# Local attention and a squared-ReLU layer on one core: another order of the opening and of block 0's first layer, with the 256-token products split by x's words

## The chip, the cores and the metric

The kernel runs on one core of one Trainium2 chip. A core has five engines that run their own instruction lists in order and wait for one another by semaphores: TensorE (PE, matrix products; its loads of weights are shown as PEld), VectorE (DVE), ScalarE (ACT), GpSimd (POOL) and SyncE (SP, which here issues nearly all DMA transfers). The metric is the device time of one execution in microseconds (us), as the median of several runs. One further execution was recorded by the profiler, and its records are the trace that the rows below come from.

## The reference, cut to what matters

```python
q, k, v: (8, 8, 576, 64) float32      # batch, heads, sequence, head size
# attention inside chunks of 64 positions
scores = (1 / sqrt(64)) * q_c @ k_c^T          # 64 x 64 in each chunk
attn = exp(scores - max); attn = attn / (attn.sum(-1) + 1e-9)
x = (attn @ v_c), laid out as (4608 tokens, 512)
# the layer
h = x @ w_in            # 512 x 2048
g = s * relu(h) ** 2 + b
out = g @ w_out         # 2048 x 512, float32
```

The weights arrive as 64-bit floats and are turned into 32-bit floats on the chip.

## The kernel before, in words

The first 512 tokens are worked by themselves (class `Layer`), the other 4096 in four blocks of 1024 (class `Block`). To keep float32 accuracy on PE, a matrix product is made of three: each operand is split into a high word and a low word (`hi` and `lo`), and high x high, high x low and low x high are summed. A product of 128 x 128 weights with 512 tokens is one PE instruction of about 0.227 us, one with 256 tokens takes about half. In the blocks of 1024 the first layer is computed with 7 products in place of 8 of half-size operands (steps p1 to p7, copies u, joins c11 to c22, relux and reluy, sqx and sqy). The first 512 tokens use plain products, and the weights come in while these run.

What stands first in time is a hand-written list of step names, `ORDER`. It is executed once from front to end, and each step appends its instructions to the lists of its engines. So the list fixes the order on every engine, and on SP the order in which transfers are issued. The steps that matter here:

- `one` and `two` are the attention groups of the first 256 + 256 tokens, each in halves 0 and 1: load_qk, load_v (512 KB transfers), scores (PE L498), peak, sub, exp, sum, normz, norm (DVE, exp on ACT), transposes (PE L559), copies (ACT L564), values (PE L571), x_hi (ACT L579) and x_lo (DVE L583). `three` to `ten` are later groups of 256 tokens in one piece (scores L395, norm L421, transposes L431, values L456). Groups three to six make the tokens of the first block of 1024: their x words are x11.hi, x21.hi, x21.lo (DVE L625) and so on.
- Weight tiles come in as `load0` to `load15`, each 1 MB (load0 in halves a and b), and each goes through ACT `scale` (L179) and `tail` (L183), DVE `shift` (L189) and `sign` (L191), POOL `add` (L197), ACT `hi` (L201) and DVE `lo` (L205). There are three buffers for them.
- `up<j>` is the first layer's product j of 16 for 512 tokens (L689, 12 products of 512 columns). `up0a` and `up1a` are its first 256 columns (the tokens of group one), `up0b` and `up1b` the second 256 (group two), 12 products of 256 columns each. Then come `relu` (ACT L694), `square` (ACT L701), `g_hi` (ACT L706) and `g_lo` (DVE L710). `down<j>` is the second layer's product j (PE L664, 12 products: 6 into `ps_x`, 6 into `ps_o`). There are two `ps_h` tiles. From j = 2 on, `g_lo` is the last reader of the one that `up` filled, so the `up` after the next waits for it.
- `s_add`, `s_hi` (ACT L245), `s_lo` (DVE L248) make the sums of weights for the 7 products; `in` and `out` store weights; `ring` loads them back.
- `keep_busy<n>` issues n products of a tile of ones with itself, 128 columns each (L131). Their result is read by nobody. The trace shows each as two passes.

In the list before, `keep_busy` stands at six places (7, 3, 8, 7, 4 and 2 products). The first layer starts with up1a, up0a, then `three.scores`, up1b, up0b, up3 and up2, and down0. After the step `nine.scores` in the middle of the list, the lists before and after the change are alike but for the order of a few neighbours up to `p3.4`.

Of the kernel before, what the change touches and what calls it, by code (L numbers as in the profile page):

```python
# [20 lines left out]
one.scores0 one.peak0 s_and_b sb one.sub0 one.exp0 one.scores1 keep_busy7 one.peak1 one.sum0 three.load_v one.sub1
one.normz0 one.norm0 one.exp1 four.load_v tail0b one.transposes0 keep_busy3 one.sum1 one.normz1 one.copies0 one.norm1
tail0a scale0a load2 one.transposes1 four.load_qk shift0a scale0b two.scores0 keep_busy8 one.copies1 sign0a shift0b
add0a two.peak0 two.sub0 hi0a sign0b two.scores1 two.exp0 lo0a add0b two.peak1 one.values0 keep_busy7 two.sum0
# [5 lines left out]
g_lo0 g_hi3 three.norm down0 scale4 g_lo1 hi3 shift4 relu2 g_lo3 three.transposes sign4 square2 g_hi2 down1 load6 lo3  # L30
tail5 scale5 add4 g_lo2 in2 three.copies up4 shift5 hi4 sign5 tail6 load7 four.scores lo4 relu4 scale6 add5 up5 out1
four.peak square4 five.load_qk g_hi4 four.sub hi5 shift6 down2 load8 g_lo4 relu5 sign6 tail7 scale7 lo5 three.values
four.exp add6 in3 square5 up6 four.sum three.x_out g_hi5 shift7 hi6 g_lo5 down3 sign7 relu6 square6 four.normz g_hi6
# [1276 lines left out]
```

## Time and profile before

| what | value |
|---|---|
| time, median of 3 runs | 781.4 us (780.26 to 781.6) |
| profiled execution, its own time | 779.79 us |
| span of that execution in the trace | 777.8 us |
| PE busy | 765.3 us, 98% of the span |
| DVE / ACT / POOL busy | 600.8 / 475.1 / 48.7 us |
| chain that ended last, by engine | PE 83%, DMA 8%, DVE 4%, ACT 3% |

The profiled execution's own time is 2.0 us above its span: the span runs from the first to the last recorded instruction. Its time lies 1.6 us under the median of the three runs. An engine counts as busy while an instruction of it runs; a row of the timeline gives the start of an instruction or of a run of like ones, its duration, the engine, the line of the kernel, the operation, what it writes and reads with the shape, the count, and in brackets the idle time just before it with what ended that idle time.

### The profile page before, as it was taken

Reading aid. Unit: us, or ns where it says so; the run is one execution under the profiler, and the core shown is the slowest. Engines: PE = TensorE matmul, PEld = TensorE weight load, DVE = VectorE, ACT = ScalarE, POOL = GpSimd, SP = SyncE. Lnnn points to the kernel's source line nnn. Section 1 sums busy time; section 2 is a strip of 40 time slices with the busy share of each in tenths; the row PEclk is TensorE's granted clock in tenths of the full one; section 3 lists DMA queues with packets and bytes.
Section 4 is the critical chain, followed back from the end, with each engine's and each line's share of the span. In section 5 each row is a group of like instructions: output and inputs, shape, how many; then the busy total and the mean of one; then the engine's idle time right before and its main releaser. Section 6 shows DMA issues by size and latency. Waiting matters only on the chain.

```text
span 777.8 us, 13753 instructions
## 1 busy us (share of the span) xinstructions
PE 765.3 (98%) x5560; PEld 632.6 (81%) x5560; DVE 600.8 (77%) x799; ACT 475.1 (61%) x657; POOL 48.7 (6%) x23
## 2 busy tenths in 40 slices
PE   6899999999999999999999999999999999999998
PEld 5788887888888888888888888888888888888886
DVE  6988899986479999889888956677998623348773
ACT  4899877867664552776764535667755345575442
POOL 1453440000000000000000000000000000000000
PEclk9999999999999999999999999999999999999999
DMA  9999999677898889999756687765575778876653
GB/s 357 352 357 344 373 302 321 231 248 222 282 386 306 305 287 367 356 321 334 232 184 223 204 319 261 268 248 190 170 236 194 236 265 284 307 256 217 212 193 136
DMA packets 86227, 211.66 MB, mean 272 GB/s; under 512 B 6036, under 2 KB 42388, under 8 KB 75924
## 3 DMA queue, kind: packets, MB, share of 16 engines
q1 hardware_dynamic: 85872, 210.53, 77.8%
q8 instruction: 44, 0.72, 0.4%
q10 hardware_dynamic: 292, 0.26, 0.1%
q14 instruction: 19, 0.16, 0.1%
HBM read 166.72 MB, written 44.04 MB: 271 GB/s over the span
## 4 chain that ended last, share of the span: by engine, by line
PE 83%; DMA 8%; DVE 4%; ACT 3%; issue 1%; SPq 1%; POOL 0%; POOLq 0%; DVEq 0%
PE ps_h L745 22%; PE ps_h L994 17%; PE ps_o L745 17%; PE ps_x L994 8%; PE ps_o L994 4%; PE ps_o L896 3%; PE ps_o L923 3%; DMA raw<-in_w_dram 3%; DMA w_in<-t 3%; PE ps_h L896 1%; PE ps_x L923 1%; PE ps_x L896 1%; PE ps_a L395 1%; DMA w_out<-t 1%; PE ps_x L456 1%; DMA t<-in_qkv_dram 1%
## 5 line engine op out<-in xcount | busy, mean ns | idle before, releaser
L745 PE MATMUL ps_h<-t,raw 128*128 128x512 f32 x672 | 167.2, 391 | 0.0
L964 DVE TENSOR_TENSOR t<-t 128x512 fp32r<-128x512 f32 (+1 forms) x140 | 123.0, 900 | 36.1 <-ACT t L959 36.1
L745 PEld LDWEIGHTS ps_h<-t,raw 128*128 128x128 f32 x672 | 125.5, 188 | 26.3
L994 PE MATMUL ps_h<-t,raw 128*128 128x512 f32 (+1 forms) x588 | 142.4, 385 | 0.0
L764 DVE TENSOR_TENSOR t<-ps_o,u 128x512 f32<-128x512 f32 x96 | 65.5, 687 | 82.2 <-PE ps_o L745 64.9
L994 PEld LDWEIGHTS ps_h<-t,raw 128*128 128x128 f32 x588 | 108.8, 188 | 22.2
L745 PE MATMUL ps_o<-t,raw 128*128 128x512 f32 x480 | 122.0, 390 | 0.0
L959 ACT CAST t<-t 128x512 fp32r<-128x512 f32 (+1 forms) x140 | 102.3, 789 | 16.0 <-DVE t L943 5.8
L745 PEld LDWEIGHTS ps_o<-t,raw 128*128 128x128 f32 x480 | 89.9, 188 | 19.0 <-DVE t L764 0.3
L755 ACT COPY u<-ps_h 128x512 f32<-128x512 f32 x96 | 55.9, 584 | 72.4 <-PE ps_h L745 72.0
L994 PE MATMUL ps_x<-t,raw 128*128 128x512 f32 x288 | 73.2, 390 | 0.0
L808 ACT ACTIVATE t<-t 128x1024 f32<-128x1024 f32 x64 | 67.1, 1052 | 0.2
L994 PEld LDWEIGHTS ps_x<-t,raw 128*128 128x128 f32 x288 | 53.9, 188 | 11.6 <-DVE shift L1166 0.3
L804 ACT ACTIVATE t<-t 128x512 f32<-128x512 f32 (+1 forms) x64 | 54.1, 847 | 12.9 <-DVE t L764 12.8
L197 POOL TENSOR_TENSOR t<-t,raw 128x1024 int32<-128x1024 int32 (+1 forms) x17 | 48.0, 2822 | 66.9 <-DVE t L191 40.7
L998 ACT ACTIVATE u<-ps_h,shift,sb 128x512 f32<-128x512 f32 x18 | 13.1, 781 | 58.2 <-PE ps_h L994 58.2
L689 PE MATMUL ps_h<-x,t 128*128 128x512 f32 (+1 forms) x216 | 47.1, 371 | 1.6 <-DVE x L583 1.6
L689 PEld LDWEIGHTS ps_h<-x,t 128*128 128x128 f32 x216 | 36.8, 188 | 8.8 <-DVE x L583 1.8
L994 PE MATMUL ps_o<-t,raw 128*128 128x512 f32 x144 | 36.5, 389 | 0.0
L443 DVE STREAM_TRANSPOSE pT<-p 32x512 f32<-32x512 f32 x48 | 33.7, 703 | 0.9
L800 ACT ACTIVATE t<-ps_h 128x512 f32<-128x512 f32 x32 | 19.1, 597 | 23.4 <-PE ps_h L745 23.4
L994 PEld LDWEIGHTS ps_o<-t,raw 128*128 128x128 f32 x144 | 27.0, 188 | 5.6
(145 smaller groups left out, 1052.2 us busy)
## 6 DMA issues: line engine op xcount, KB each, us to landing
raw<-w_in SPq DMA_DIRECT2D x42, 1024.0 KB, 6.0
raw<-w_out SPq DMA_DIRECT2D x29, 1024.0 KB, 5.1
raw<-w_sum SPq DMA_DIRECT2D x28, 1024.0 KB, 5.2
raw<-in_w_dram SPq DMA_DIRECT2D x15, 1024.0 KB, 7.7
qk<-in_qkv_dram SPq DMA_DIRECT2D x15, 1024.0 KB, 9.1
w_out<-t SPq DMA_DIRECT2D x16, 512.0 KB, 6.9
t<-w_out SPq DMA_DIRECT2D x16, 512.0 KB, 7.9
w_sum<-t SPq DMA_DIRECT2D x16, 512.0 KB, 7.6
```

The lines of the kernel that those rows point to most:

```text
L197: nc.gpsimd.tensor_tensor(out=i, in0=i, in1=low.bitcast(I32), op=ALU.add)
L443: nc.vector.transpose(out=self.pT[cols, 1 - k], in_=p[rows, k])
L689: nc.tensor.matmul(out=self.ps[j][:, cols], lhsT=w[:, c, :], rhs=x[:, c, :], start=(c == 0 and i == 0), stop=(c == NHP - 1 and i == 2))
L745: nc.tensor.matmul(out=ps, lhsT=w[:, e, :], rhs=y[:, e, :], start=start and e + i == 0, stop=e + i == 3, skip_group_check=not start)
L755: nc.scalar.copy(out=u, in_=self.a[p])
L764: nc.vector.tensor_tensor(out=self.tile(p, h)[:, e, :], in0=ps, in1=u, op=ALU.add)
L804: nc.scalar.activation(out=t, in_=t, func=AF.Relu)
L808: nc.scalar.activation(out=t, in_=t, func=AF.Square)
L896: nc.tensor.matmul(out=self.acc[names[m // 2]][m % 2], lhsT=x, rhs=y, start=j == 0 and q == 0, stop=q == 2, skip_group_check=j > 0)
L959: nc.scalar.copy(out=hi, in_=f)
L964: nc.vector.tensor_tensor(out=lo, in0=f, in1=hi.bitcast(F32), op=ALU.subtract)
L994: nc.tensor.matmul(out=self.acc[name][m][:, cols], lhsT=x, rhs=y[:, cols], start=new and q == 0, stop=q == 2, skip_group_check=not new)
```

## The change

Three things change. The list `ORDER` is rewritten from its start up to the step `nine.scores`. `Layer.up` takes the three products in the order high x high, low weight x high x, high weight x low x (before: the low word of x second, the low word of the weights third), and can issue a part of them. And the four 256-column steps are split: `up<j>a.x` and `up<j>b.x` issue the first two products of each of the four chunks (8 instructions, which read no low word of x), `.y` the third (4 instructions). `keep_busy` stands at four places: 8 products ahead of everything, then 13, 10 and 11. The count of real products is the same.

```diff
 ORDER = """
-one.load_qk0 one.load_qk1 load0b one.load_v load0a two.load_qk0 two.load_qk1 load1 two.load_v three.load_qk
...
-one.x_hi0 two.sub1 load3 hi0b one.x_lo0 two.exp1 lo0b one.values1 keep_busy4 tail1 two.normz0 in0 two.sum1 one.x_hi1
-scale1 two.norm0 two.normz1 two.transposes0 keep_busy2 two.norm1 one.x_lo1 shift1 two.copies0 two.values0 sign1
-two.transposes1 two.x_hi0 two.copies1 add1 two.x_lo0 up1a scale2 tail2 two.values1 shift2 up0a hi1 sign2 two.x_hi1
-three.scores lo1 add2 two.x_lo1 in1 three.peak scale3 up1b tail3 three.sub up0b open_o load4 relu1 shift3 hi2 up3
...
+keep_busy8 one.load_qk0 one.scores0 one.peak0 s_and_b sb one.sub0 one.exp0 one.load_qk1 load0b two.load_qk0 load0a two.load_qk1
+two.load_v one.load_v load1 three.load_v load2 one.scores1 keep_busy8 keep_busy5 one.peak1 one.sub1 one.sum0 scale0b
...
+two.sub1 one.x_hi0 load3 tail1 two.exp1 hi0b two.normz0 two.norm0 two.sum1 lo0b one.values1 two.transposes0 keep_busy9
+two.normz1 scale1 keep_busy2 two.copies0 tail2 one.x_hi1 shift1 two.norm1 two.values0 sign1 one.x_lo0 one.x_lo1
+two.transposes1 add1 up1a.x up1a.y two.x_hi0 scale2 two.copies1 two.x_lo0 up0a.x two.values1 three.scores up0a.y
+two.x_hi1 hi1 shift2 sign2 add2 two.x_lo1 three.peak three.sub up1b.x up1b.y relu1 scale3 up0b.x up0b.y open_o load5
...
-eight.normz u2.3 s_keep4 eight.norm p2.4 u1.4 eight.turn p6.4 p7.3 c11.4 u2.4 eight.swap0 relux.4 p7.4 u3.3 c22.3 p4.3
-u3.4 eight.swap1 p3.3 ring9 c21.3 sqx.3 p1.5 s_hi5 c12.3 p4.4 ring10 s_lo5 u1.5 reluy.3 p5.4 s_keep5 c21.4 sqy.3
-eight.values nine.scores c22.4 sqx.4 p3.4 eight.x_out nine.load_v nine.peak p6.5 nine.sub s_hi6 ring11 c12.4 p2.5
...
+eight.swap0 relux.4 p7.4 u3.3 c22.3 p4.3 u3.4 ring8 p4.4 p3.3 ring9 c21.3 sqx.3 c12.3 p5.4 eight.values ring10 c21.4
+reluy.3 sqy.3 s_hi5 s_lo5 s_keep5 p1.5 u1.5 nine.scores c22.4 sqx.4 p3.4 eight.x_out nine.load_v nine.peak p6.5
...
-        def up(self, j, cols=slice(0, HALF)):
+        def up(self, j, cols=slice(0, HALF), part=(0, 1, 2)):
...
-                for i, (w, x) in enumerate(((h, xh), (h, xl), (l, xh))):
-                    nc.tensor.matmul(out=self.ps[j][:, cols], lhsT=w[:, c, :], rhs=x[:, c, :],
-                                     start=(c == 0 and i == 0), stop=(c == NHP - 1 and i == 2))
+                for i, (w, x) in enumerate(((h, xh), (l, xh), (h, xl))):
+                    if i in part:
+                        nc.tensor.matmul(out=self.ps[j][:, cols], lhsT=w[:, c, :], rhs=x[:, c, :],
+                                         start=(c == 0 and i == 0), stop=(c == NHP - 1 and i == 2))
...
-        named["up%da" % j], named["up%db" % j] = partial(layer.up, j, first), partial(layer.up, j, second)
+        for h, cols in (("a", first), ("b", second)):
+            named["up%d%s" % (j, h)] = partial(layer.up, j, cols)
+            named["up%d%s.x" % (j, h)], named["up%d%s.y" % (j, h)] = partial(layer.up, j, cols, (0, 1)), partial(layer.up, j, cols, (2,))
```

In the changed file the lines of `Layer` stand one lower: L690 is `up`, L711 is `g_lo`.

First place: PE from the last scores of group two to the first `down`. L498 are scores of one and two, L559 transposes, L571 values, L131 the products of keep_busy (a count of products, not passes), L395 `three.scores`. Before:

```order
L498 MATMUL ps_p<-t 64x64 x16
L571 MATMUL ps_p<-pT,t 64x64 x16
L131 MATMUL ps_h<-t 128x128 x7
L571 MATMUL ps_p<-pT,t 64x64 x16
L131 MATMUL ps_h<-t 128x128 x4
L559 MATMUL ps_a<-ident,t 128x128 x4
L131 MATMUL ps_h<-t 128x128 x2
L571 MATMUL ps_p<-pT,t 64x64 x16
L559 MATMUL ps_a<-ident,t 128x128 x4
L689 MATMUL ps_h<-x,t 128x256 x12
L571 MATMUL ps_p<-pT,t 64x64 x16
L689 MATMUL ps_h<-x,t 128x256 x12
```

In the changed kernel:

```order
L571 MATMUL ps_p<-pT,t 64x64 x16
L559 MATMUL ps_a<-ident,t 128x128 x4
L131 MATMUL ps_h<-t 128x128 x11
L571 MATMUL ps_p<-pT,t 64x64 x16
L559 MATMUL ps_a<-ident,t 128x128 x4
L690 MATMUL ps_h<-x,t 128x256 x20
L571 MATMUL ps_p<-pT,t 64x64 x16
L395 MATMUL ps_a<-t 64x64 x32
L690 MATMUL ps_h<-x,t 128x256 x28
L690 MATMUL ps_h<-x,t 128x512 x24
```

The 11 warming products now stand between group two's two sets of transposes; 20 products of 256 columns (up1a.x, up1a.y, up0a.x) run ahead of the last values and of `three.scores`, and 28 behind.

Second place: DVE around `shift8`, `sign8`, `lo6`, `shift9` and `g_lo7`. L205 is `lo`, L189 `shift`, L191 `sign`, L710 `g_lo`. Before:

```order
L421 TENSOR_TENSOR t<-t,z 128x1024
L205 TENSOR_TENSOR t<-t 128x1024
L189 TENSOR_SCALAR t<-t 128x1024
L205 TENSOR_TENSOR t<-t 128x1024
L191 SCALAR_TENSOR_TENSOR t<-raw,t 128x1024
L189 TENSOR_SCALAR t<-t 128x1024
L710 TENSOR_TENSOR t<-ps_h,t 128x512
```

In the changed kernel:

```order
L421 TENSOR_TENSOR t<-t,z 128x1024
L205 TENSOR_TENSOR t<-t 128x1024
L189 TENSOR_SCALAR t<-t 128x1024
L191 SCALAR_TENSOR_TENSOR t<-raw,t 128x1024
L205 TENSOR_TENSOR t<-t 128x1024
L189 TENSOR_SCALAR t<-t 128x1024
L711 TENSOR_TENSOR t<-ps_h,t 128x512
```

`sign8`, after which POOL may start `add8`, and `lo6` have changed places; `shift9` and `g_lo7` follow as before.

Third place: DVE around `sign12`, `five.norm` (L421) and `x21.lo` (L625), up to the step `lo11` (the last L205 here). Before:

```order
L189 TENSOR_SCALAR t<-t 128x1024
L421 TENSOR_TENSOR t<-t,z 128x1024
L191 SCALAR_TENSOR_TENSOR t<-raw,t 128x1024
L625 TENSOR_TENSOR t<-half,t 128x1024
L710 TENSOR_TENSOR t<-ps_h,t 128x512 x2
L625 TENSOR_TENSOR t<-half,t 128x1024
L189 TENSOR_SCALAR t<-t 128x1024
L205 TENSOR_TENSOR t<-t 128x1024
```

In the changed kernel:

```order
L189 TENSOR_SCALAR t<-t 128x1024
L191 SCALAR_TENSOR_TENSOR t<-raw,t 128x1024
L421 TENSOR_TENSOR t<-t,z 128x1024
L625 TENSOR_TENSOR t<-half,t 128x1024
L711 TENSOR_TENSOR t<-ps_h,t 128x512 x2
L625 TENSOR_TENSOR t<-half,t 128x1024
L189 TENSOR_SCALAR t<-t 128x1024
L205 TENSOR_TENSOR t<-t 128x1024
```

`sign12` now stands ahead of `five.norm`, so two more operations with two operands in the core's memory (the norm and `x21.lo`) follow it. In the same way `sign15` and `lo14` now stand ahead of `six.norm`, and PE's `six.transposes` ahead of `down12`.

## Rows read from the trace of the kernel before

**Rows 1.** Windows: busy us (x instructions) of each engine, granted clock, DMA share, GB/s.
```profile
0.00:36.00 36.00, 27.07 (x459) 24.21 (x460) 28.37 (x46) 22.62 (x32) 10.30 (x11) 1.00 0.94 354
36.00:774.40 738.40, 738.27 (x5103) 608.42 (x5101) 571.90 (x753) 452.47 (x626) 38.37 (x13) 1.00 0.78 269
```

**Rows 2.** Timeline of PE in the opening: start, duration, instruction, idle before.
```profile
6.91 2.65 PE L131 MATMUL ps_h<-t 128*128 128x128 f32 x14
...
22.64 0.69 PE L571 MATMUL ps_p<-pT,t 64*64 64x64 f32 x32 [0.28 <-ACT pT L564]
...
23.68 1.68 PE L689 MATMUL ps_h<-x,t 128*128 128x256 f32 x12
...
30.82 8.47 PE L689 MATMUL ps_h<-x,t 128*128 128x256 f32 x47 [1.60 <-DVE x L583]
39.13 1.67 PE L664 MATMUL ps_x<-t 128*128 128x512 f32 x6
```

**Rows 3.** Timeline of DVE in the opening.
```profile
12.66 0.43 DVE L189 TENSOR_SCALAR t<-t 128x512 uint32<-128x512 uint32 x1 [0.78 <-ACT t L179]
...
20.46 0.68 DVE L529 TENSOR_TENSOR t<-t,z 128x512 f32<-128x512 f32 x1
...
26.05 1.72 DVE L189 TENSOR_SCALAR t<-t 128x1024 uint32<-128x1024 uint32 x1 [0.80 <-ACT t L179]
...
30.08 0.69 DVE L583 TENSOR_TENSOR x<-ps_p,x 128x512 fp32r<-128x512 f32 x1
...
33.08 0.68 DVE L189 TENSOR_SCALAR t<-t 128x1024 uint32<-128x1024 uint32 x1
...
36.07 1.21 DVE L414 TENSOR_REDUCE z<-t 128x16 f32<-128x1024 f32 x1
...
38.69 0.63 DVE L710 TENSOR_TENSOR t<-u,t 128x512 fp32r<-128x512 f32 x1
```

**Rows 4.** The chain that ended last, the transfer of load2.
```profile
11.19 13.63 DMA raw<-in_w_dram
```

**Rows 5.** Timeline of POOL: `add1`, `add8`.
```profile
24.78 2.44 POOL L197 TENSOR_TENSOR t<-t,raw 128x1024 int32<-128x1024 int32 x1 [6.95 <-ACT pT L564]
...
69.15 2.69 POOL L197 TENSOR_TENSOR t<-t,raw 128x1024 int32<-128x1024 int32 x1 [5.59 <-DMA raw<-in_w_dram]
```

**Rows 6.** Timeline of DVE at the second place, `g_lo7` and `sign9`.
```profile
69.45 0.68 DVE L710 TENSOR_TENSOR t<-ps_h,t 128x512 fp32r<-128x512 f32 x1
70.06 2.88 DVE L191 SCALAR_TENSOR_TENSOR t<-raw,t 128x1024 uint32<-128x1024 uint32 x1
```

**Rows 7.** Timeline of PE: `up9`; `up13`; `down12`.
```profile
71.25 2.88 PE L689 MATMUL ps_h<-x,t 128*128 128x512 f32 x12
...
97.73 1.66 PE L689 MATMUL ps_h<-x,t 128*128 128x512 f32 x6
...
115.50 1.52 PE L664 MATMUL ps_x<-t 128*128 128x512 f32 x6
```

**Rows 8.** Timeline of DVE at the third place.
```profile
90.66 1.22 DVE L625 TENSOR_TENSOR t<-half,t 128x1024 fp32r<-128x1024 f32 x1
93.97 1.29 DVE L710 TENSOR_TENSOR t<-ps_h,t 128x512 fp32r<-128x512 f32 x2 [2.10 <-ACT t L706]
...
96.92 1.22 DVE L205 TENSOR_TENSOR t<-t 128x1024 fp32r<-128x1024 f32 x1
```

**Rows 9.** Timeline of DVE: `six.norm`, `lo14`.
```profile
110.36 1.22 DVE L421 TENSOR_TENSOR t<-t,z 128x1024 f32<-128x1024 f32 x1
...
112.63 1.22 DVE L205 TENSOR_TENSOR t<-t 128x1024 fp32r<-128x1024 f32 x1
```

**Rows 10.** Groups by line and shape: count, busy, mean ns, idle before.
```profile
L764 DVE TENSOR_TENSOR t<-ps_o,u 128x512 f32<-128x512 f32 x96 | 65.5, 687 | 82.2 <-PE ps_o L745 64.9 <-ACT u L755 13.6 <-ACT t L800 1.9
...
L804 ACT ACTIVATE t<-t 128x1024 f32<-128x1024 f32 x32 | 34.0, 1061 | 11.1 <-DVE t L764 11.1
...
L248 DVE TENSOR_TENSOR x<-t,x 128x1024 fp32r<-128x1024 f32 x8 | 9.7, 1220 | 0.6 <-ACT x L245 0.6
```

More of the change, by code (lines that the diff above doesn't have):

```diff
@@ L19 @@
 ORDER = """
-one.load_qk0 one.load_qk1 load0b one.load_v load0a two.load_qk0 two.load_qk1 load1 two.load_v three.load_qk
[L21 to L24, printed above, removed]
@@ L30 @@
[L30 to L33, printed above, removed]
-load9 add7 tail8 g_lo6 up7 scale8 four.norm hi7 lo7 four.transposes relu7 square7 load10 shift8 up8 scale9 in4 lo6
@@ L35 @@
-four.copies sign8 g_hi7 tail9 down4 shift9 out2 add8 g_lo7 relu8 square8 tail10 up9 g_hi8 sign9 load11 hi8 g_lo8 add9
-scale10 down5 relu9 square9 g_hi9 shift10 hi9 lo8 five.scores sign10 out3 down6 scale11 load12 five.peak six.load_qk
-add10 tail11 g_lo9 five.sub down7 hi10 shift11 lo9 five.exp sign11 in5 four.values lo10 tail12 up11 add11 five.sum
-scale12 load13 five.load_v out4 four.x_out five.normz hi11 up10 shift12 five.norm x21.hi relu11 sign12 x11.hi down8
-x21.lo relu10 square11 add12 square10 load14 g_hi11 g_hi10 five.transposes g_lo11 scale13 g_lo10 down9 five.copies
@@ L40 @@
-x11.lo hi12 shift13 lo11 tail13 six.scores sign13 in6 up13 lo12 scale14 add13 six.peak load15 out5 tail14
-seven.load_qk six.sub up12 relu13 square13 shift14 ring0 six.exp s_add1 hi13 down10 sign14 relu12 g_hi13 lo13 square12
-tail15 add14 g_lo13 five.values in7 g_hi12 six.sum scale15 down11 g_lo12 five.x_out six.normz shift15 hi14 six.load_v
-six.norm up14 sign15 ring1 lo14 up15 add15 out6 relu14 square14 g_hi14 g_lo14 hi15 down12 s_add0 ring2 s_hi1 lo15
-s_hi0 s_add7 relu15 six.transposes out7 square15 down13 g_hi15 s_add5 six.copies s_lo0 six.values s_lo1 s_keep0 g_lo15
@@ new lines @@
+three.transposes load6 lo3 g_lo2 g_lo3 tail5 scale5 add4 in2 three.copies up4 hi4 shift5 sign5 load7 four.scores lo4
+relu4 square4 tail6 g_hi4 scale6 add5 up5 four.peak five.load_qk load8 out1 g_lo4 four.sub tail7 hi5 shift6 sign6
+down2 relu5 lo5 three.values add6 in3 four.exp square5 g_hi5 scale7 up6 four.sum three.x_out g_lo5 shift7 sign7 relu6
+square6 four.normz g_hi6 load9 add7 tail8 hi6 g_lo6 up7 down3 four.norm hi7 scale8 lo7 four.transposes relu7 square7
+load10 shift8 sign8 up8 scale9 in4 lo6 g_hi7 relu8 square8 tail9 g_hi8 tail10 four.copies down4 shift9 out2 add8 g_lo7
@@ new lines @@
+scale10 up9 sign9 load11 add9 g_lo8 hi8 hi9 relu9 square9 g_hi9 scale11 shift10 lo8 five.scores down5 sign10 load12
+out3 down6 down7 five.peak five.sub six.load_qk add10 tail11 g_lo9 hi10 shift11 sign11 lo9 tail12 scale12 four.values
+lo10 add11 load13 in5 load14 five.load_v out4 four.x_out five.exp five.sum x11.hi five.normz hi11 up11 up10 shift12
+sign12 five.norm x21.hi relu11 square11 relu10 down8 x21.lo add12 g_hi11 square10 g_hi10 five.transposes g_lo11
+scale13 g_lo10 down9 five.copies x11.lo hi12 shift13 lo11 six.scores sign13 up13 six.peak six.sub lo12 scale14 tail13
@@ new lines @@
+add13 ring0 load15 out5 in6 up12 down10 tail14 relu13 hi13 square13 shift14 six.exp s_add1 sign14 relu12 g_hi13 lo13
+square12 g_hi12 tail15 add14 five.values in7 g_lo12 six.sum scale15 down11 g_lo13 five.x_out shift15 six.normz hi14
+six.load_v ring1 seven.load_qk up14 sign15 lo14 six.norm up15 add15 out6 relu14 square14 g_hi14 g_lo14 hi15 s_add0
+lo15 s_hi1 s_add7 six.transposes down12 down13 s_hi0 s_lo0 s_add5 six.copies relu15 square15 six.values s_lo1 s_add6
+down14 p1.0 s_keep1 six.x_out g_hi15 g_lo15 xt1.add_dve xt1.hi xt3.add_dve x22.hi seven.scores seven.load_v ring2
```

60 lines of the change are left out of this document (32 added, 28 removed).

## The prediction

> **What bounds the kernel now.** I read the windows first [rows 1]. From 36 us to PE's last instruction at 774.4 PE is busy 738.27 of 738.40 us: behind the opening there is no idle time to win. The granted clock is 1.00 in both windows. So the end comes earlier only by what the first 36 us lose of their idle time, 36.00 − 27.07 = 8.9 us, and later by every new wait behind them. The next view is PE's timeline of the opening [rows 2]. PE reaches `down0` at 39.13. Its largest late wait is 1.60 us before the 47 products from 30.82, put down to x_lo (L583). DVE's timeline says why that word is late [rows 3]: the last x_lo starts at 30.08 behind shift2 (26.05), which waited 0.80 us for ACT's scale2 and then took 1.72 us; a like shift takes 0.68 at 33.08. Scale2 waited for load2, whose transfer took 13.63 us from 11.19 and landed at 24.82 [rows 4].
>
> The stretch of 1.72 matters for everything below. POOL's add1 runs from 24.78 for 2.44 us [rows 5], to 27.22, and the shift that starts at 26.05 ends only at 27.77, some 0.55 after add1: about 1.0 us of standing still. At 70.06 sign9 takes 2.88 us beside add8, where other DVE operations of its size with two operands in the core's memory take 1.22 [rows 6, 8]. Add8 itself, started at 69.15 while shift9 ran, took 2.69 instead of 2.44. So the trace shows DVE and POOL excluding each other for a whole instruction: the one that comes second stands still.
>
> **The Trainium skill on this.** "SBUF — State Buffer", section "Who interferes with whom", says the same: a VectorE operation with two SBUF inputs, or in a 2-port mode, and a GpSimd operation that reads SBUF share one pair of ports, and the one that issues first locks the other out. The trace agrees (1.72 against 0.68). It speaks against any order that puts such operations right behind the `sign` that releases an `add`.
>
> **The opening: a gain.** DVE's list reaches the end of two.norm0 at about 20.46 + 0.60 = 21.06 now [rows 3]. In the new list x_lo0, lo0b and two.sum1, 0.6 us each from one start to the next, stand behind it, and the 0.78 wait at 12.66 is filled: 21.06 − 1.8 − 0.78 = 18.5. On PE follow two.transposes0 (about 0.45), 11 warming products in 22 passes of 0.11 us (2.45), values (0.6, [rows 2]), transposes (0.45) and 0.1 of hand-overs: up1a starts at about 22.5 instead of 23.68 [rows 2].
>
> From there PE has 48 products of 256 columns, 24 of 512, the last values and three.scores. The 8.31 us from 30.82 to 39.13 hold 23 of the one and 24 of the other, which 0.124 and 0.227 us each fill. So 5.95 + 5.45 + 0.6 + 1.17 = 13.2. Today the same stretch takes 39.13 − 23.68 = 15.45, since it holds the 1.60 wait. Does it go? Load2 stands 1.5 MB further forward in SP's queue; at 410 KB per us, the rate of the full slices (the mean of 354 holds the slow start), it lands 3.8 us earlier, near 21.0. The values of group two's second half end at about 25.7, its x_hi at 26.4, its x_lo at 27.2; the first product that reads it (up1b.y) starts after 32 products of 256 columns, values and scores, 22.5 + 4.0 + 1.8 = 28.3. So the wait goes, with 1 us to spare, and 0.3 is left for hand-overs and for `lo1`, which up3 wants at its second product now. `down0` could start at 22.5 + 13.2 + 0.3 = 36.0, a gain of 3.1. I take **−3.0**, with −2.3 (up1a only 0.7 earlier and x_lo just in time) and −3.6 as ends.
>
> **The rows behind it: the lead is spent.** A PE that is 3 us ahead gains only if what it waits for comes 3 us earlier too.
>
> - *down0* reads g_lo0. Three.sum, which stands at 36.07 for 1.21 us [rows 3], now stands ahead of g_lo0 on DVE with no normz between them, and itself waits for three.exp on ACT, which is hardly earlier (about 34.9 to 35.0). So sum ends at 36.2, g_lo0 at 36.8 against 36.1 wanted: **+0.6** (0.3 to 0.9).
> - *Second place (add8).* Today sign8 is followed by shift9, then add8 runs beside g_lo7, which reads PSUM and isn't stopped. g_lo7 ends at 70.13 and up9, which takes its tile, starts at 71.25: 1.12 us to spare [rows 6, 7]. In the new list lo6 runs behind sign8, add8 waits for it, and then add8 and shift9 want the same thing at the same moment. If POOL goes first, shift9 stands still for about 2.2 us and g_lo7 is late by 2.2 − 1.12 = 1.1. DVE comes there a little earlier against PE than now: **+0.8** (0 to 1.2).
> - *Third place (add12).* After the rewritten order add12 starts when five.norm ends, and x21.lo stands still for its 2.2 us. Today DVE has 2.10 us idle ahead of 93.97 [rows 8], which would have let it follow an earlier PE; that is used up. up13 starts at 97.73 [rows 7] and reads lo11 (96.92 + 1.22 = 98.14, [rows 8]) in its third product; now in its second, 0.23 us earlier, so there is no slack left. Of the 1.6 us of lead that are left by then about 1.0 is lost, and the 0.23: **+1.2** (0.2 to 1.8).
> - *add15.* Six.norm stands at 110.36 today, ahead of sign15 and lo14 [rows 9]. Now it stands behind both, and add15's 2.2 us fall on one of the two. Started at 110.36, sign15, add15, then the last of the two and its partner end the norm at 110.36 + 1.14 + 2.3 + 2.4 = 116.2. Six.transposes, which reads it, stands where down12 stands today, at 115.50 [rows 7], and down12 no longer covers it: **+1.0** with hand-overs (0 to 1.3).
> - *The words xt1 to xt4 near 136 us.* Two differences and two `lo` stand one behind the other on DVE now: **+0.3** (0 to 0.5).
> - *p3.4 near 183 us.* It waits for c22.4, which now stands behind s_lo5 on DVE, and s_lo5 behind reluy.3, sqy.3 and s_hi5 on ACT. From c12.3 (0.69) through the three ACT operations (1.06 each; one form stands in the rows, the other two are alike), s_lo5 (1.22) and c22.4 (0.69) this is 5.8 us [rows 10]. PE has p5.4, eight.values, p1.5 and nine.scores to do meanwhile, 1.36 + 1.1 + 1.36 + 1.1 = 4.9: **+0.9**, whatever the lead (0.5 to 1.2).
>
> Sum: −3.0 + 0.6 + 0.8 + 1.2 + 1.0 + 0.3 + 0.9 = **+1.8**. The profiled execution ran 779.79, so its like would be 781.6. The median of the three runs is 781.4, 1.6 above the profile; against it the forecast is **783.1**.
>
> Edits costed at nothing: the product order itself adds no product. The 8 warming products in front run before the first transfer lands (4.48 us of PE idle lie there); without that cover they would cost 16 passes, some 3 us. SP's moved stores (in0, in1 behind load3 to load5) have no reader before `ring0`, past 100 us.
>
> **The rivals.**
> 1. *DVE goes first.* No row of before shows DVE and POOL asking at the same moment, so who wins is not known. If DVE's next instruction, already in its queue, goes first, then add8, add12 and add15 wait instead, and nothing in PE's way stands still. Left are down0 0.6, p3.4 0.9, near 136 0.3, and some 1.4 of the lead that DVE can't follow: about +0.2, 781.6, nothing to measure. For it: shift9 behind sign8 today went first, but POOL had not asked yet.
> 2. *The lead stays: faster.* POOL loses every contest, and DVE's and ACT's lists move forward with the loads, so that only down0's stall and a part of p3.4's come: −3.0 + 0.8 = −2.2, 779.2. It decides itself at g_lo0: if three.exp ends by 34, down0 starts at 36.1. Against it: p3.4's sum doesn't depend on the lead.
> 3. *The 13 products behind the first scores run slowly: slower still.* At 6.91 fourteen passes took 2.65 us, 0.189 each [rows 2], against 0.11 later. If the 8 in front don't change that, 26 passes take 4.9 us from 6.9 to 11.8, where one.norm0 is ready near 10.9; the opening loses up to 0.9 more: 784.0.
>
> **How the numbers follow.** About 0.2% (1.6 us) is what a measurement of this kernel can tell from no change: 779.8 to 783.0. My forecast has 0.46, and its stalls' ends put 0.30 of that above 783.0 and 0.16 inside. Rival 1 has 0.26 (0.22 inside, 0.02 on each side, rounded), rival 2 0.17 (all faster but 0.01), rival 3 0.11 (0.10 slower). That gives faster 0.18, same 0.40, slower 0.42. The range goes from rival 2's value, 779.3, to 785.0, which is rival 3 with a second place at its upper end; the forecast's own is 782.0 to 784.6.
>
> **What would show it.** Right: `down0` near 36.1 to 36.8 with a wait for g_lo0; a shift or norm of 2.5 to 3.4 us on DVE beside add8, add12 and add15; PE idle of 0.7 to 1.3 near 68, 96 and 114, and 0.9 near 183 before p3.4. The lead can be read at any later PE row as the difference to its row today: −3 at 36, about 0 at 115, +1 at 185. Wrong: POOL's adds stretched by two operations instead of DVE's (rival 1); no PE idle after 37 (rival 2); passes of 0.19 us after 7 us (rival 3); or load2 landing after 23, which would leave the 1.60 wait where it is.

## The result and the profile after

The changed kernel takes 788.32 us in the median (788.3 to 789.62, 5 runs) against 781.6 for the kernel before (780.26 to 782.4, 5 runs): a ratio of 1.009, 95% interval 1.0076 to 1.0105. It is slower by 6.7 us; 783.1 was forecast, and 785.0 was the upper end of the range. The profiled execution took 788.31 us, span 786.2, which is 8.4 above the span of before; the profiled execution of before lay 1.8 us under its own median, and that is the difference between 8.4 and 6.7. What follows is counted in the spans.

Windows of the changed kernel (busy us and instructions of PE, PEld, DVE, ACT, POOL; granted clock, DMA share, GB/s):

```profile
0.00:36.00 36.00, 32.19 (x490) 28.98 (x491) 27.77 (x47) 23.02 (x33) 10.60 (x11) 1.00 0.94 360
36.00:60.00 24.00, 19.63 (x205) 15.29 (x204) 21.53 (x21) 20.37 (x29) 9.05 (x4) 1.00 0.98 334
...
200.00:782.80 582.80, 581.99 (x3699) 480.98 (x3697) 433.20 (x580) 325.48 (x449) 0.00 (x0) 1.00 0.75 260
```

In the first 36 us PE is busy for 5.1 us more than in [rows 1] (part of it warming products). Behind them, where before had 0.13 us of idle time in 738, it stands idle 4.4 us in the next 24 alone. Its waits behind 36 us, by what released them:

```profile
PE ps_h L690 <- DVE t L205: 2.9, 2, 2.0
PE ps_h L690 <- DVE t L711: 2.8, 2, 2.0
PE ps_a L431 <- DVE t L421: 1.3, 1, 1.3
PE ps_h L746 <- issue: 0.8, 1, 0.8
PE ps_o L746 <- DVE t L765: 0.6, 1, 0.6
PE ps_x L664 <- DVE t L711: 0.4, 1, 0.4
```

The same waits in order of time, with the start of `down0` in the first line:

```profile
36.99 0.39 PE L664 MATMUL ps_x<-t 128*128 128x512 f32 x1
37.74 1.43 PE L664 MATMUL ps_x<-t 128*128 128x512 f32 x5 [0.37 <-DVE t L711]
...
46.13 3.01 PE L690 MATMUL ps_h<-x,t 128*128 128x512 f32 x12 [2.00 <-DVE t L711]
...
59.44 5.52 PE L690 MATMUL ps_h<-x,t 128*128 128x512 f32 x23 [2.00 <-DVE t L205]
...
74.84 3.01 PE L690 MATMUL ps_h<-x,t 128*128 128x512 f32 x12 [0.79 <-DVE t L711]
...
102.82 5.51 PE L690 MATMUL ps_h<-x,t 128*128 128x512 f32 x23 [0.87 <-DVE t L205]
...
121.81 1.06 PE L431 MATMUL ps_a<-ident,t 128*128 128x128 f32 x8 [1.28 <-DVE t L421]
...
189.74 1.65 PE L746 MATMUL ps_o<-t,x 128*128 128x512 f32 x6 [0.61 <-DVE t L765]
...
350.83 0.73 PE L746 MATMUL ps_h<-t,raw 128*128 128x512 f32 x2 [0.78 <-issue]
```

These are down0, up4, up6, up9, up13, six.transposes, p3.4 and a pause in the third block. The bracket understates a wait, since a row lasts to the end of its last product: the single one at 36.99 lasts 0.39 us, where the next would start 0.227 us later. Counted from one start to the next, less the usual time of what stands before them (0.227 us for a product of 512 columns), the first seven cost 0.52, 2.2, 2.3, 0.97, 1.14, 1.4 and 0.67 us; the pause costs 1.0, the difference of the two traces at their ends (8.4) less that at p3.4 (189.74 − 182.35 = 7.4). With down0 2.14 us earlier than in [rows 2] this makes −2.14 + 10.2 = 8.1 of the 8.4. The rest is seen at a row of 18 like products that stands some 13 us ahead of p3.4 in both traces, here before the change, the row and then p3.4:

```profile
169.35 4.24 PE L745 MATMUL ps_h<-t,x 128*128 128x512 f32 x18
...
182.35 1.66 PE L745 MATMUL ps_o<-t,x 128*128 128x512 f32 x6
```

The changed kernel has that row at 175.26, so from it to p3.4 it takes 14.48 us where before takes 13.00, for the same products: 0.67 is the wait, and the other 0.8 comes without one, where eight.values and nine.scores no longer stand side by side. Some 0.5 us had been won between 120 and 170 us.

Whose operation is late is read from DVE and from POOL. DVE, in order: lo3, lo5, shift9, x21.lo, six.norm:

```profile
42.00 3.48 DVE L205 TENSOR_TENSOR t<-t 128x1024 fp32r<-128x1024 f32 x1 [0.17 <-ACT t L201]
...
56.52 2.87 DVE L205 TENSOR_TENSOR t<-t 128x1024 fp32r<-128x1024 f32 x1 [0.86 <-ACT t L201]
...
71.23 2.95 DVE L189 TENSOR_SCALAR t<-t 128x1024 uint32<-128x1024 uint32 x1
...
95.23 3.47 DVE L625 TENSOR_TENSOR t<-half,t 128x1024 fp32r<-128x1024 f32 x1
...
118.21 3.46 DVE L421 TENSOR_TENSOR t<-t,z 128x1024 f32<-128x1024 f32 x1
```

And POOL's add4, add6, add8, add12, add15:

```profile
41.96 2.43 POOL L197 TENSOR_TENSOR t<-t,raw 128x1024 int32<-128x1024 int32 x1 [5.07 <-ACT t L201]
...
55.88 2.42 POOL L197 TENSOR_TENSOR t<-t,raw 128x1024 int32<-128x1024 int32 x1 [3.91 <-DMA qk<-in_qkv_dram]
...
70.40 3.23 POOL L197 TENSOR_TENSOR t<-t,raw 128x1024 int32<-128x1024 int32 x1 [4.76 <-ACT t L179]
...
94.41 3.20 POOL L197 TENSOR_TENSOR t<-t,raw 128x1024 int32<-128x1024 int32 x1 [4.75 <-DVE t L191]
...
117.38 3.20 POOL L197 TENSOR_TENSOR t<-t,raw 128x1024 int32<-128x1024 int32 x1 [3.07 <-DMA w_in<-t]
```

Each of the five DVE operations takes 1.6 to 2.3 us more than usual and ends 0.5 to 1.1 us after the add beside it, that is a little less than its usual duration. For the first two POOL simply began first, add4 by 0.04 us; its 2.43 are its usual time [rows 5]. In the other three POOL asked while an earlier DVE operation ran (its 3.2 hold that wait), and then went ahead of DVE's next one. (A sixth place of this kind, lo10 with 3.44 us at 87.30 behind add11, makes PE wait for nothing.) Before the change lo3 came first, and add4 waited for it; lo3, then add4:

```profile
43.65 1.22 DVE L205 TENSOR_TENSOR t<-t 128x1024 fp32r<-128x1024 f32 x1
```

```profile
43.87 3.31 POOL L197 TENSOR_TENSOR t<-t,raw 128x1024 int32<-128x1024 int32 x1 [5.41 <-DVE t L191]
```

ACT shows why lo3 and lo5 came second; these are hi3, then tail7 and hi5:

```profile
40.93 1.04 ACT L201 CAST t<-t 128x1024 fp32r<-128x1024 f32 x1
...
54.39 1.17 ACT L183 ACTIVATE raw<-raw 128x1024 int32<-128x1024 uint32 x1 [1.42 <-DMA raw<-in_w_dram]
55.44 1.04 ACT L201 CAST t<-t 128x1024 fp32r<-128x1024 f32 x1
```

hi3 ends at 41.97, one hundredth after add4 has begun: sign4, which releases add4, starts 1.9 us earlier than before (40.61 against 42.52), hi3 only 0.25 (40.93 against 41.18). hi5 stands behind tail7, which waits 1.42 us for load7, and add6 begins meanwhile.

### The profile page after: what moved, and what is told of

It reads as the page before. It is cut to its first block, busy times and chain, and to the rows that moved or that the text cites. A ratio compares the mean times of both kernels' runs of the same rounds, so it can differ in the third digit from the quotient of the medians.

```text
span 786.2 us, 13779 instructions
## 1 busy us (share of the span) xinstructions
PE 770.2 (98%) x5582; PEld 635.8 (81%) x5582; DVE 609.5 (78%) x799; ACT 475.4 (60%) x657; POOL 45.5 (6%) x23
## 4 chain that ended last, share of the span: by engine, by line
PE 84%; DVE 6%; DMA 5%; ACT 2%; issue 2%; SPq 0%; POOL 0%; DVEq 0%; ACTq 0%
PE ps_h L746 21%; PE ps_h L995 17%; PE ps_o L746 17%; PE ps_x L995 8%; PE ps_o L995 4%; DMA raw<-in_w_dram 3%; PE ps_o L897 3%; PE ps_o L924 3%; DVE t L205 2%; PE ps_h L897 1%; PE ps_a L395 1%; PE ps_x L924 1%; PE ps_x L897 1%; PE ps_h L690 1%; PE ps_x L456 1%
## 5 line engine op out<-in xcount | busy, mean ns | idle before, releaser
L690 PE MATMUL ps_h<-x,t 128*128 128x512 f32 (+1 forms) x216 | 47.7, 373 | 6.2 <-DVE t L205 3.1
L197 POOL TENSOR_TENSOR t<-t,raw 128x1024 int32<-128x1024 int32 (+1 forms) x17 | 44.8, 2632 | 74.5 <-DVE t L191 18.3
L690 PEld LDWEIGHTS ps_h<-x,t 128*128 128x128 f32 x216 | 36.8, 188 | 14.6 <-DVE t L205 4.1
L999 ACT ACTIVATE u<-ps_h,shift,sb 128x512 f32<-128x512 f32 x18 | 13.1, 779 | 58.2 <-PE ps_h L995 58.2
```

The lines of the kernel that those rows point to most:

```text
L197: nc.gpsimd.tensor_tensor(out=i, in0=i, in1=low.bitcast(I32), op=ALU.add)
L690: nc.tensor.matmul(out=self.ps[j][:, cols], lhsT=w[:, c, :], rhs=x[:, c, :], start=(c == 0 and i == 0), stop=(c == NHP - 1 and i == 2))
```

## The experiments

The runs were timed in four groups, each on one chip beside the kernel before, whose median there was 782.04 us (runs 1 to 4), 781.78 (5 to 8), 782.11 (9 to 12) and 781.39 (13 to 16). A run was timed 4 to 12 times. Ratios are those on record against that kernel before; they can differ by 0.1% from the quotient of the two medians.

**1. The new opening alone.** The changed list up to `down0`, then the steps left in the old order:

```diff
 ... changed list up to: three.normz shift4 g_lo1 three.norm down0
-relu2 sign4 square2 tail4 hi3 square3 g_hi2 g_hi3 down1 three.transposes load6 lo3 g_lo2 g_lo3 ...
+square3 tail4 g_hi3 hi3 relu2 g_lo3 three.transposes sign4 square2 g_hi2 down1 load6 lo3 ...
```

> The changed list up to the step down0, then the remaining steps in the order of the list before (product order and split steps as changed). Theory P (the loss lies behind down0, where five POOL adds hold DVE up: lo3 by add4, lo5 by add6, shift9 by add8, x21.lo by add12, six.norm by add15): the opening's lead of 2.1 us at down0 stays but for the 0.5 us wait for g_lo0; no wait of PE over 0.5 us behind 40 us; 779.8 to 780.4 us against 781.6 before. Rival L (the opening itself, by its moved transfers and stores or by the new product order, makes later steps late): waits of PE of 1 to 2 us come back at 46 and 59 us in spite of the old order; 783 us or more.

782.62 us; ratio 1.0016 (1.0004 to 1.0028). The waits at up4 and up6 are gone, against rival L, but theory P's gain isn't there either. Two rows of PE, and a window, show what this execution lost:

```profile
15.85 3.98 PE L132 MATMUL ps_h<-t 128*128 128x128 f32 x20
...
65.95 1.06 PE L432 MATMUL ps_a<-ident,t 128*128 128x128 f32 x8 [1.70 <-DVE t L422]
```

```profile
16.00:20.00 4.00, 4.00 (x35) 3.88 (x39) 3.30 (x8) 2.94 (x5) 1.57 (x1) 0.63 1.02 417
```

In this execution the granted clock fell in the opening and 20 warming passes took 3.98 us instead of 2.50, so down0 came at 38.02. And what was left of the lead, 0.5 us, was lost in the wait before four.transposes at 65.95. The clock is not the reason for the run's time, though: three of its twelve executions have a mean granted clock of 1.000, which leaves no room for such a fall, and their median is 782.58, that of the other nine 782.66.

**2. The new order behind `down0` alone.** The list before up to `down0`, then the changed order; product order as before:

```diff
 ... list before up to: three.normz tail4 g_lo0 g_hi3 three.norm down0
-scale4 g_lo1 hi3 shift4 relu2 g_lo3 three.transposes sign4 ...
+scale4 shift4 g_lo1 relu2 sign4 square2 hi3 g_hi2 down1 three.transposes load6 lo3 ...
```

> The list before up to down0, then the remaining steps in the changed order; product order as before. Theory P: the waits behind the adds come without the opening's help, less the slack that the steps have against a PE that is 2 us later: 785 to 789 us, with DVE operations of 2.3 to 3.5 us beside add8, add12 and add15. Rival L: without the new opening the waits at up4 and up6 are gone and at most 1 us is lost: 781.6 to 782.6 us.

787.32 us; ratio 1.0078 (1.0063 to 1.0092), 5.3 us above its own before. So nearly the whole loss lies behind down0. lo3 and lo5 start first here, and the waits at up4 and up6 don't come; those at down0, up9, up13, six.transposes and p3.4 do, at up13 and six.transposes with 1.77 and 1.90 us.

**3. One pair exchanged in the kernel before.**

```diff
-scale9 in4 lo6 four.copies sign8 g_hi7
+scale9 in4 sign8 four.copies lo6 g_hi7
```

> The kernel before, with sign8 and lo6 exchanged and nothing else. Theory P: add8 waits for lo6 and then goes ahead of shift9, which takes 2.3 to 3.0 us; g_lo7 is 2.2 us late, up9 has 1.1 us to spare: PE waits 0.8 to 1.2 us near 71 us; 782.4 to 782.8 us against 781.6. Rival (DVE's next operation goes first): shift9 takes 0.7 us, no wait, 781.6 us.

783.08 us; ratio 1.002 (1.0009 to 1.0031). Shift9 in its profile:

```profile
69.10 2.94 DVE L189 TENSOR_SCALAR t<-t 128x1024 uint32<-128x1024 uint32 x1
```

PE waits 0.85 us at up9. So POOL goes first when it asked during DVE's operation. (A later wait of 1.26 us at 124.85, for a copy of ACT, was not expected; it is also in the profiles of runs 10 and 16, 1.81 and 1.47 us, whose lists have no such exchange, and not in that of before. So the run's 1.0 us above its own before is not a clean price of the pair.)

**4. The five adds left out.** The five weight tiles lose the low word's share:

```diff
-add4 ... add6 ... add8 ... add12 ... add15
```

> The changed kernel without add4, add6, add8, add12 and add15: these five weight tiles lose the low word's share. Theory P: lo3, lo5, shift9, x21.lo and six.norm take their usual 0.7 and 1.2 us; the five waits of PE (2.2, 2.3, 1.0, 1.1 and 1.4 us measured from the end of the product before) go, the waits for g_lo0 and c22.4 stay: 780 to 781 us. Rival L (ACT's hi3 and hi5 stand too late in the new order, and POOL only happens to run then): the waits at 46 and 59 us stay at 1 us or more each; 783 us or more.

783.98 us; ratio 1.0025 (1.0008 to 1.0042), 4.3 us under the changed kernel. Lo3, lo5, shift9, x21.lo and six.norm take 0.68 to 1.23 us again, and the waits at up4, up9, up13 and six.transposes are gone. Theory P's time, 780 to 781, was missed by 3 us: in this profile the granted clock was 0.66 and 0.50 between 12 and 20 us, down0 came only at 39.17, and up4's place is not a fair test with so late a PE (run 5 is). At up6 1.7 us stay, and the rows name ACT:

```profile
57.98 0.50 PE L690 MATMUL ps_h<-x,t 128*128 128x512 f32 x1 [0.98 <-ACT t L201]
59.24 5.55 PE L690 MATMUL ps_h<-x,t 128*128 128x512 f32 x23 [0.76 <-DVE t L205]
```

So up9, up13 and six.transposes are POOL's; at up6 hi5, behind tail7, which waits 2.43 us for load7 here, is late by itself, as rival L had it.

**5. lo3 and lo5 first.**

```diff
-relu3 g_hi1 g_lo0 three.normz shift4 g_lo1 three.norm down0 relu2 sign4 square2 tail4 hi3 square3
+relu3 g_hi1 hi3 g_lo0 three.normz shift4 g_lo1 three.norm down0 relu2 sign4 square2 tail4 square3
-tail7 hi5 shift6
+hi5 tail7 shift6
```

> The changed list with two steps of ACT moved, so that lo3 and lo5 are ready before POOL asks: hi3 right behind g_hi1, hi5 ahead of tail7. Theory P: lo3 and lo5 take 1.2 us again (3.48 and 2.87 in the changed kernel), the waits of PE at up4 and up6 (2.2 and 2.3 us) shrink to under 0.5 each; the later three stay or grow by 0.5, since PE comes there earlier: 784 to 786 us against 788.3 for the changed kernel. Theory D (the transfers don't land earlier, whatever PE's lead: DMA engines are 94 to 100% busy from 5 to 60 us): the lead is lost to waits for load7 or what hangs on it before 70 us, 786.5 us or more.

786.67 us; ratio 1.0055 (1.0034 to 1.0075). lo3 and lo5 take 1.22 us each. The wait at up4 falls to 0.25, that at up6 to 0.93 (lo5). Less comes of it than P's 784 to 786: PE now waits 0.38 before four.transposes and 0.90 at up9.

**6. All five places in order.** As before, and:

```diff
-shift8 sign8 up8 scale9 in4 lo6 g_hi7
+shift8 lo6 sign8 up8 scale9 in4 g_hi7
-shift12 sign12 five.norm x21.hi
+shift12 five.norm sign12 x21.hi
-six.normz hi14 six.load_v ring1 seven.load_qk up14 sign15 lo14 six.norm up15
+six.normz six.norm hi14 six.load_v ring1 seven.load_qk up14 sign15 lo14 up15
```

> As the run before, and the other three places put back in order too: lo6 ahead of sign8, five.norm ahead of sign12, six.norm ahead of sign15 and hi14. Theory P: all five DVE operations take their usual time; of the waits behind 40 us only that for c22.4 (0.6) and at most 1 us in small ones stay; 779.5 to 781.5 us, no slower than the kernel before. Theory D: PE waits of 1 to 2 us by load7, near 55 to 66 us; 782 us or more.

784.37 us; ratio 1.0033 (1.0017 to 1.0048). No wait over 0.62 us is left, and it is still 2.6 us slower than before. down0 starts at 37.34, 1.8 us earlier than in [rows 2], and four.transposes at 65.36, where before has them at 64.80 (first line; the second is ACT's tail7 in run 6, the third the stretch from 45 to 63 us):

```profile
64.80 1.07 PE L431 MATMUL ps_a<-ident,t 128*128 128x128 f32 x8
```

```profile
54.67 1.23 ACT L183 ACTIVATE raw<-raw 128x1024 int32<-128x1024 uint32 x1 [1.21 <-DMA raw<-in_w_dram]
```

```profile
45.00:63.00 18.00, 17.81 (x193) 13.95 (x194) 14.56 (x19) 16.67 (x23) 9.53 (x4) 1.00 1.02 379
```

The lead is gone there without a large wait of PE, but ACT waits 1.21 us for load7. At four.transposes the run is 0.6 us behind before, and its span ends 3.6 us longer. At the row of 18 products ahead of p3.4 it is 1.4 us behind (170.75 against 169.35), at p3.4 2.85 (185.20 against 182.35), and the pause near 346 us adds 0.8. So p3.4's place and the pause, which no edit of this run touches, make up most of what is left.

**7. Warming products moved into the gaps.**

```diff
-one.norm1 one.transposes0 ... one.transposes1 four.load_qk four.load_v one.values0 keep_busy8 keep_busy2
+one.norm1 keep_busy4 one.transposes0 ... one.transposes1 keep_busy8 four.load_qk four.load_v one.values0 keep_busy2
```

> As the run before, and 8 of the 10 warming products moved ahead of the values that wait for one.v, 4 more put ahead of one.transposes0, so that PE has no gap over 0.6 us from 5 to 20 us. Theory C (gaps of 1.2 to 1.4 us in the new opening let the granted clock fall to half: 0.63 and 0.50 in 16 to 20 us in two profiles, where 20 passes took 3.98 us instead of 2.50): granted clock 1.00 throughout the opening, down0 reached by 37.2 us, 0.5 to 1.5 us less than the run before. Rival (the clock of those profiles was chance of the execution, nothing to do with the gaps): no difference to the run before.

785.06 us; ratio 1.0038 (1.0022 to 1.0054). No difference to the run before that can be told: the clock stayed at 1.00 in the opening in both profiles, so theory C isn't tested. A wait of 1.19 us at up9 came, and a pause of 1.81 us in the third block, behind which the granted clock was 0.57 from 348 to 352 us. A lead need not be lost by four.transposes, as this trace shows; tail7, then four.transposes:

```profile
53.03 1.18 ACT L184 ACTIVATE raw<-raw 128x1024 int32<-128x1024 uint32 x1 [0.97 <-DMA raw<-in_w_dram]
```

```profile
63.69 1.06 PE L432 MATMUL ps_a<-ident,t 128*128 128x128 f32 x8 [0.28 <-DVE t L422]
```

They start 1.1 us earlier than before, with nothing left out. In runs 6 and 7 alike they follow tail7's start by 10.7 us, and tail7 waits for load7 in both.

**8. Without the 8 products in front.**

```diff
-keep_busy8 one.load_qk0 one.scores0
+one.load_qk0 one.scores0
```

> The changed kernel without the 8 warming products in front of everything. If these bring the clock up for what follows: the 26 passes from 7 us take about 5 us instead of 3.17, the first transposes start near 12 instead of 11.26, down0 is 0.3 to 1.5 us later, 789 to 790 us. If they do nothing: passes as before at 0.12 us, 788.3 us.

788.41 us; ratio 1.0081 (1.0053 to 1.0109). The 26 passes behind the first scores, here and then in the changed kernel:

```profile
6.93 4.80 PE L131 MATMUL ps_h<-t 128*128 128x128 f32 x26
```

```profile
7.16 3.17 PE L131 MATMUL ps_h<-t 128*128 128x128 f32 x26
```

Behind the front products a pass takes 0.122 us in place of 0.185. That the clock does it is not shown: the granted clock reads 1.00 from 4 to 12 us in both traces. PE then waits 0.93 us for one.norm0 instead, and only 0.34 us is gained at down0 (36.99 against 37.33). The equal times do not price the front products, for this trace has no pause near 345 us, but a longer wait at up4 and a granted clock of 0.50 from 48 to 50 us behind it, where up4 takes 4.61 us instead of 3.01:

```profile
47.21 4.61 PE L690 MATMUL ps_h<-x,t 128*128 128x512 f32 x12 [2.74 <-DVE t L711]
```

**9 and 10. The stores in0 moved.** In the kernel of run 6 six stores went forward, in the kernel before twelve went back:

```diff
-load5 load4 in0
+lo0b in0 ... load5 load4
```

```diff
-two.normz0 in0 ... two.x_lo1 in1 ... open_o load4
+two.normz0 ... two.x_lo1 ... open_o load4 in0 in1
```

> The kernel with the five places in order, and the six stores in0 issued right behind lo0b, ahead of load5 and load4, as in the kernel before. Theory D (the stores, issued between 31 and 41 us instead of 18 to 32, share the DMA engines with load6 and load7; tail7 waits 1.2 us for load7, and exp of group four stands behind it on ACT): load7 lands 1 to 2 us earlier, the wait of 1.2 us on ACT goes, 0.5 to 1.5 us less than 784.4. Rival (the transfers as a whole are the limit, so the place of the stores doesn't matter): no change, 784.4 us.

> The kernel before, with the stores in0 and in1 issued behind load4 and nothing else. Theory D: tail6 or tail7 waits 1 to 2 us longer for its load near 45 to 55 us, four.transposes near 65 us come 0.5 to 1.5 us later, 782.3 to 783.5 us against 781.8. Rival: the 1.5 MB of stores have room elsewhere, 781.8 us.

784.28 us, ratio 1.0022 (1.0008 to 1.0035), and 782.01 us, ratio 1.0005 (0.9991 to 1.002). Neither time differs from that of the kernel it was made from. Theory D, as the place of these stores, is not borne out in the times; in run 9 tail7 no longer waits for load7, but the wait for a load only moved (1.85 us on ACT at 38.92), and in run 10's profile four.transposes do come 0.7 us later (65.46), as D had it.

**11. Runs 1 and 9 together,** with six of ten warming products in front of one.values0.

> The first run's kernel (changed list up to down0, old order behind), with in0 early and with six of the ten warming products moved into PE's wait for one.v. If the lead of the opening can be kept with the stores out of the way and the clock up: down0 by 37.2 us, PE's wait near 66 us (1.7 us in the first run) under 0.7, 780.0 to 781.3 us, the fastest of all. If loads set the pace up to 66 us: the wait stays over 1 us, 781.5 to 783 us.

782.89 us; ratio 1.0011 (0.9997 to 1.0026): no faster than before. The clock fell to 0.59 between 20 and 24 us, down0 came at 38.71, four.transposes at 66.45.

**12. The x split in the kernel before.**

```diff
-scale3 up1b tail3 three.sub up0b
+scale3 up1b.x up0b.x up1b.y tail3 three.sub up0b.y
```

> The list before with one thing of the change alone: the new product order, and the 24 products of group two's columns issued as up1b.x, up0b.x, up1b.y, up0b.y, so that 16 products that read no low word cover x_lo. The wait of 1.60 us for x_lo then falls to under 0.3, and down0 comes 1.3 to 1.6 us earlier (37.6). If what follows can come earlier too: 780.2 to 780.5 us. If loads and ACT set the pace up to 66 us: the lead is lost in a wait before four.transposes, 781.8 us.

781.53 us; ratio 0.9995 (0.9979 to 1.0011). The wait for x_lo is gone, but a wait of 0.72 for ACT's relu comes ahead of up3, so down0 starts at 38.34, only 0.8 earlier. Its second product waits for g_lo0:

```profile
39.38 1.43 PE L664 MATMUL ps_x<-t 128*128 128x512 f32 x5 [0.65 <-DVE t L711]
```

In [rows 2] that product starts 0.227 behind 39.13, at 39.36: the lead is spent inside down0, and three.transposes start at 42.01 as before (42.02). four.transposes start at 65.26, behind a wait of 0.51.

**13 and 14. Less work on the weights.** Runs 6 and 12 without tail6, add6, tail7 and add7 (two weight tiles lose the low word's share):

```diff
-tail6 ... add6 ... tail7 ... add7
```

> The changed list with the five places in order, without tail6, add6, tail7 and add7: two weight tiles lose the low word's share, ACT has 2.2 us less to do between 45 and 65 us and four.norm no longer stands behind add6. Theory A (ACT's and DVE's work on the weights sets when four.transposes start): they start 1 to 2 us earlier than 65.36 and PE keeps 1 us or more of its 1.8 us lead there; 782 to 783.3 us against 784.4. Rival (the transfers set it): 65 us and 784.4 us as before.

> The list before with group two's products split (the run before the last one's fellow, down0 0.8 us earlier than in the kernel before), without tail6, add6, tail7 and add7. Theory A: no wait before four.transposes (0.51 us with them), these start near 64.0; PE's lead of 0.8 us stays to the end, 780.7 to 781.0 us. Rival: 65.2 us, 781.5 us.

783.81 us, ratio 1.002 (1.0005 to 1.0036), and 780.76 us, ratio 0.9991 (0.9977 to 1.0005). The times don't settle it: run 13 lies 2.4 us above its own before where run 6 lay 2.6, run 14 0.6 below its own where run 12 lay 0.6 below. The profiles say more; four.transposes in run 6, then in run 13:

```profile
65.36 1.07 PE L431 MATMUL ps_a<-ident,t 128*128 128x128 f32 x8 [0.40 <-DVE t L421]
```

```profile
63.43 1.03 PE L431 MATMUL ps_a<-ident,t 128*128 128x128 f32 x8
```

down0 starts at 37.34 and 37.46 in these two; with 2.2 us less on ACT and without add7 beside four.norm PE arrives 1.9 us earlier. This does not tell theory A from its rival: tail7 is the step that waits 1.21 us for load7 in run 6, and four.exp stands behind it, so leaving it out takes away the work and the wait for the transfer at once. The lead of 1.4 us over before then lasts to the row of 18 products ahead of p3.4 (169.35 before) and is gone at p3.4 (182.35 before):

```profile
168.50 4.24 PE L746 MATMUL ps_h<-t,x 128*128 128x512 f32 x18
...
182.95 1.66 PE L746 MATMUL ps_o<-t,x 128*128 128x512 f32 x6 [0.60 <-DVE t L765]
```

It is 0.85 us at the first, and p3.4's place costs 1.45, as in every trace of the changed order (1.45 to 1.7); a pause of 0.9 follows. Run 14 tests nothing of the lead, since run 12's is spent in down0; four.transposes start at 64.71 there. The kernel before has a nearly full ACT between 45 and 63 us:

```profile
45.00:63.00 18.00, 18.00 (x197) 14.61 (x196) 14.89 (x18) 17.71 (x25) 10.56 (x4) 1.00 0.96 347
```

ACT is busy 17.71 of 18.00 us there, beside a PE that is busy all the time, and tail7 waits for no transfer (53.91). In run 6 ACT is busy 16.67. So what holds tail7 back differs from list to list; what is common is that four.transposes follow tail7's start by 10.6 to 11.1 us in before and in runs 1, 3, 5 to 7, 9 to 12, 15 and 16 (11.6 to 13.1 in the changed kernel and in runs 2, 4 and 8).

**15. The work moved, nothing left out.** Run 12 with three.copies on DVE:

```diff
-three.copies      # nc.scalar.copy
+three.copies_dve  # nc.vector.tensor_copy
```

> The list before with group two's products split, and three.copies done by DVE instead of ACT, so that ACT has 1.1 us less in the full stretch; nothing is left out. Theory A: four.transposes start near 64.3 and 0.5 to 0.8 us of the lead stay: 780.8 to 781.3 us, the fastest of the complete kernels. Rival: DVE's 1.3 us more make its own chain late: 781.5 us or more.

781.27 us; ratio 1.0004 (0.9989 to 1.0019). ACT is down to 15.81 us in that stretch, but it now waits 1.16 and 0.49 us there for POOL's adds, tail7 starts at 54.71, 0.8 later than before, and four.transposes come at 65.62 behind four.norm. As in run 12, no lead reaches three.transposes (42.01), so nothing could be kept.

**16. The 8 products in front of the kernel before.**

```diff
+keep_busy8
 one.load_qk0 one.load_qk1 load0b
```

> The kernel before with the 8 warming products in front and nothing else (16 more PE passes). If the pause of PE near 346 us in the changed kernel goes with the number of PE instructions ahead: a pause of 0.5 to 1 us appears near 340 to 345 us, 782.5 to 783 us. If it goes with the new list: none, 781.8 us. The seven products at 6.9 us take about 1.6 instead of 2.65 us if the front ones bring the clock up.

783.1 us; ratio 1.0018 (1.0001 to 1.0035). The 14 passes take 1.83 us in place of 2.65, and PE then waits longer for one.norm0 (1.74). The pause came, but not where it was expected:

```profile
18.05 0.26 PE L571 MATMUL ps_p<-pT,t 64*64 64x64 f32 x1 [1.78 <-issue]
```

## Why the prediction was wrong

The direction was right, and so was the mechanism of the stalls; the sum was short by two places of the same kind, and by the pause.

- **The step that failed** is the list of stalls under "the rows behind it": it has no term for lo3 beside add4 and lo5 beside add6. They were put at nothing without a reason. Their places on DVE are the same in both lists, but what decides is which comes first, the `hi` on ACT that releases the `lo` or the `sign` that releases the add. sign4 came 1.9 us earlier and hi3 0.25; hi5 stands behind tail7 and load7. So POOL began first and held DVE for 3.48 and 2.87 us: 2.2 + 2.3 = 4.5 us at up4 and up6 that the sum didn't have. Run 5 shows it (with the two `hi` moved lo3 and lo5 take 1.22 us, the waits 0.25 and 0.93). Of the 2.3 at up6 1.65 is POOL's (2.87 less 1.22), and the other 0.6 is hi5's own lateness.
- **The stalls that were forecast** came: g_lo0 0.52 (forecast 0.6), add8 0.97 (0.8), add12 1.14 (1.2), add15 1.4 (1.0), p3.4 0.67 (0.9). At p3.4 another 0.8 came without a wait. The one near 136 us did not come as a wait in the changed kernel. Without up4, up6 and the pause the sum would have come to about +2.9 us against the forecast +1.8. (That forecast has two slips of 0.1: 781.4 and 1.8 make 783.2, and rival 2's value is 779.2.)
- **The opening** gave 2.14 instead of 3.0. two.norm0 ended at 18.37, where 18.5 was forecast, but up1a started at 23.02 and not at 22.5: the work between took some 0.3 us longer, and at its end PE waited for one.x_hi1 on ACT, which stands behind tail2 and so behind load2 (row below, with two.x_hi0). up3 waited 0.26 for lo1, which stands behind three.peak and three.sub.

```profile
22.40 1.05 ACT L579 CAST x<-ps_p 128x512 fp32r<-128x512 f32 x2
```

- **That the lead counts in full at the end** was no error in this trace, where −2.14 enters the sum as it stands. But once stalls are taken out the lead mostly doesn't last. When down1 and three.transposes are done, runs 1, 5, 6 and 9 are 0.4 to 1.5 us ahead of before; at four.transposes they are 0.5 to 1.2 us behind it (65.29 to 65.95 against 64.80). In run 7 1.1 us are left there, and in run 13, with less work on ACT, 1.4. four.transposes hang on tail7 on ACT; whether ACT's work or the landing of load7 holds tail7 back is not the same in all lists, and the cause stays open.
- **A pause of 1.0 us** in the third block was not forecast (below).
- **The rivals.** That DVE goes first is refuted by run 3. That the lead stays and the kernel is faster is refuted by the time. The slow passes behind the first scores didn't come in the changed kernel (3.17 us for 26), and in run 8, where they came, down0 lost only 0.3.

The Trainium skill's rule on the shared ports ("SBUF — State Buffer", "Who interferes with whom") held in all five places: the one that issues first locks the other out for the whole instruction. What decided here is who issues first, by 0.04 us at add4.

With all five places in order (run 6) the ratio falls from 1.009 to 1.0033, so they account for well over half of the loss. No version beat the kernel before by more than the measurement can tell; the best complete ones are runs 12 and 15.
